# A delta-rule attention with a hard-swish MLP on one core: VectorE's order in the first five steps placed anew

## The chip, the core and the metric

The kernel runs on one core of a Trainium2 chip. The core has TensorE (PE; its weight loads are a row of their own, PEld), VectorE (DVE), ScalarE (ACT) and GpSimd (POOL), and DMA queues that here are issued from SyncE's queue (SP) and ScalarE's queue (ACTq). Each engine works its instructions off in the order of the program and waits for others by semaphores. The metric is the device time of one execution in microseconds (us).

## The reference

```python
def _attn_ref(q, k, v, beta):                 # B, H, S, D = 4, 8, 768, 48
    k_n = k / (np.linalg.norm(k, axis=-1, keepdims=True) + 1e-06)
    state = np.zeros((B, H, D, D))
    for t in range(S):
        y[:, :, t] = np.einsum('bhd,bhde->bhe', q[:, :, t], state)
        v_old = np.einsum('bhde,bhd->bhe', state, kt)
        state = state + bt * np.einsum('bhd,bhe->bhde', kt, vt - v_old)
    return y
def _moe_ref(x, w_in, w_out):                 # x is y as 3072 tokens x 384; d_ff = 2048
    h = x @ w_in
    g = h * np.clip(h + 3.0, 0.0, 6.0) / 6.0
    return g @ w_out
```

Inputs and output are 32-bit floats, but the two weight matrices arrive as 64-bit floats.

## The kernel before, in words

**Chunks.** The 768 steps of the recurrence are cut into 24 chunks t of 32 steps, and four chunks make a group g. A chunk holds 128 rows (4 batches x 32 steps) and all 8 heads. `norms(g, i0, n)` works out the inverse norms of n chunks: squares `sq` of k, a sum `ss` by VectorE, and 13 small VectorE operations (a seed, three Newton rounds, a reciprocal) up to `inv`. There is one buffer for `sq`, so a square waits for the sum of the one before. `prep(t)` has three stages: POOL makes `kb` (k times inv), the mask `mb` and `bkb`; PE transposes `kb` and then `qb` into PSUM (`pt`) and ACT copies each to `KQ`; PE makes the scores `sc` and VectorE multiplies them by `mb` to `LB`, which goes to `l_dram`. `inverse(g)` fetches the four chunks' triangles into `A`, inverts them in 30 steps on VectorE (a product `pr` and a subtraction into `A` in each), writes them to `x_dram` and fetches them back into the four `LB`. `chain(t)` is the serial part: `ks` and part of `py` from the state, `R` (VectorE), `pz`, `Z` (ACT), the rest of `py`, `y` (ACT), the update `su` with `state` (VectorE), and `yt`, which puts y transposed into `xT`.

**Weights.** w_in comes in 8 pieces of 256 columns, w_out in 8 pieces of 256 rows (0 to 7 and 8 to 15 below). A raw piece `d` is loaded by SP and made a 32-bit float by `convert` in five VectorE operations (`e`, `m`, `m`, `e`, and the last one into `w_in` or `w_out`) and one of ACT; each VectorE operation is a step that the program can place. Raw pieces and the k of a group share three buffers.

**MLP.** Two chunks make a block of 256 tokens. A unit of `up` is one of 16 column tiles: three products into `ph`, ACT's `t`, VectorE's `g`; one piece of w_in serves two units. A unit of `down` is two products into `po` by w_out. `ph`, `po`, `pt`, `pz` and `yt` share four PSUM buffers.

**Order.** Nothing reorders the work beyond the program's own order: under `manual_schedule` the loops at the end call the generators step by step (`take`, `drain`), and `need(n)` runs `convert` until n pieces are done. First come chunks 0 to 3 with `norms` of group 1 between them, then `inverse(0)` with the preparation of chunks 4 to 7 between its steps, then `chain(0)` and `chain(1)`. In the steps t = 2 and 3 each has 8 units of `up(0)`; in between lie `chain(t)` and `fill`, which is `norms(2)` and `inverse(1)`. From t = 4 on, `down` begins.

Of the kernel before, what the change touches and what calls it, by code (L numbers as in the profile page):

```python
# [17 lines left out]
def kernel(  # L18
# [28 lines left out]
    GS = 4  # L47
# [154 lines left out]
    def norms(g, i0, n):  # L202
# [3 lines left out]
        for i in range(n):  # L206
            sq = work.tile([P, H, D], FP32, name="sq", bufs=1)
            if g == 0:
                nc.scalar.activation(out=sq[:], in_=kf[:, i0 + i], func=ACTF.Square)
            else:  # L210
                nc.gpsimd.tensor_tensor(  # L211
                    out=sq[:], in0=kf[:, i0 + i], in1=kf[:, i0 + i], op=ALU.mult
                )
            nc.vector.tensor_reduce(out=ss[:, i, :], in_=sq[:], axis=AX.X, op=ALU.add)  # L214
            yield
# [277 lines left out]
    def mlp_units():  # L493


        u1 = up(1)
        yield from up(0)
        for f in range(0, NFC, WF):
            for c in range(CB):
                need(NWI + f // WF + 1)  # L500
                down(0, c, f, WF)
                yield
            for _ in range(WF):
                next(u1)
                yield
        for blk in range(1, N // CB):
            for c in range(CB):
                for f in range(0, NFC, 2):
                    down(blk, c, f, 2)
                    yield  # L510
            if blk + 1 < N // CB:
                yield from up(blk + 1)
# [27 lines left out]
    with tc.manual_schedule():  # L540
        with tc.tile_pool(name="early", bufs=3) as early:
# [5 lines left out]
            load_w(0, early)  # L547
# [7 lines left out]
            for t in range(1, GS):  # L555
# [3 lines left out]
                take(inv1, 3)  # L559
                take(first[t])  # L560
            drain(inv1)
            load_w(1, early)
            load_v(0)
            load_v(1)
            load_w(2, early)
            load_w(3)
            need(1)
            inv = inverse(0, nc.scalar)
            take(inv)
            for t in range(GS):  # L570
                take(prep_of(GS + t))
                take(inv, 4)
                take(prep_of(GS + t), 2)
                if t < 2:
                    take(prep_of(GS + t))
            load_w(4)
            take(inv, 4)
            take(conv)
            drain(inv)
            for t in range(2, GS):  # L580
                take(prep_of(GS + t))
            need(2)
# [6 lines left out]
            need(3)  # L589
# [3 lines left out]
        for t in range(CB, N):  # L593
# [29 lines left out]
            for u in range(NU):  # L623
# [4 lines left out]
                if early:  # L628
                    need(min(NWI, ((t - CB) * NU + u) // 4 + 1))
                else:  # L630
                    take(conv, 2)
                take(units)
                take(fill, 3 if early else 1 + (u % 2 == 0))
# [32 lines left out]
```

## Time and profile before

| what | value |
| --- | --- |
| median of 3 timed runs | 805.8 us (804.25 to 805.96) |
| the profiled execution's own time | 803.47 us |
| span of its trace | 801.8 us |
| PE busy in the span | 681.7 us (85%) |
| VectorE busy | 356.3 us (44%) |
| ScalarE busy, GpSimd busy | 181.9 us, 93.1 us |

The profiled execution took 1.67 us more than its trace spans, which is what lies around the first and the last instruction. PE is busy all the time from 245 us on; before that it has gaps.

### The profile page before, as it was taken

What the parts mean: (1) busy time and instruction counts of PE and PEld (TensorE: products, weight loads), DVE (VectorE), ACT (ScalarE), POOL (GpSimd) and SP (SyncE); (2) the same over time, 40 slices, a digit from 0 to 9 for tenths busy, and PEclk for the clock granted to TensorE, in tenths of its full rate; (3) what the DMA queues carried; (4) which work ended last, traced back from release to release, by engine and by line L of the source; (5) the groups of instructions that cost most, each with busy time, mean ns of one, the idle gap of its engine ahead of it and who ended that gap; (6) DMA issues with size and microseconds to landing.
All of it is one profiled execution on the core that took longest, in us unless ns stands there. A gap on an engine that the chain in (4) does not pass through costs nothing.

```text
span 801.8 us, 24917 instructions
## 1 busy us (share of the span) xinstructions
PE 681.7 (85%) x11208; PEld 502.7 (63%) x11208; DVE 356.3 (44%) x865; ACT 181.9 (23%) x357; POOL 93.1 (12%) x138
## 2 busy tenths in 40 slices
PE   0351483457879999999999999999999999999997
PEld 0341462335657687686786776876867768677684
DVE  3379547675862872136751248711366202112020
ACT  0221120122232032131131320322312203112120
POOL 2561012000300301004002012010000000000000
PEclk9996586578999999999999999999999999999999
DMA  6354651225742114250132330121201200000000
GB/s 120 72 121 103 146 109 32 74 72 125 211 80 46 39 23 83 42 110 8 30 69 40 62 71 12 47 46 38 52 12 48 38 14 19 8 17 1 20 1 20
DMA packets 140140, 45.77 MB, mean 57 GB/s; under 512 B 130273, under 2 KB 133345, under 8 KB 140033
## 3 DMA queue, kind: packets, MB, share of 16 engines
q1 hardware_dynamic: 127008, 41.18, 22.6%
q10 hardware_dynamic: 13024, 2.98, 1.8%
q8 instruction: 88, 1.44, 0.8%
q14 instruction: 20, 0.16, 0.1%
HBM read 33.13 MB, written 11.01 MB: 55 GB/s over the span
## 4 chain that ended last, share of the span: by engine, by line
PE 76%; DVE 13%; DMA 4%; SPq 2%; issue 2%; POOL 1%; ACT 1%; ACTq 0%; POOLq 0%; DVEq 0%
PE po L481 31%; PE ph L460 31%; DVE A L324 3%; DVE pr L320 3%; PE pz L372 2%; PE py L372 2%; PE su L429 2%; PE pt L275 2%; PE ks L362 2%; SPq L85 2%; PE sc L288 2%; PE py L362 1%; DMA qb<-in_q_dram 1%; DVE m L179 1%; DVE e L183 1%
## 5 line engine op out<-in xcount | busy, mean ns | idle before, releaser
L460 PE MATMUL ph<-xT,w_in 128*128 128x256 f32 x1152 | 278.8, 395 | 43.4 <-DVE w_in L188 36.9
L460 PEld LDWEIGHTS ph<-xT,w_in 128*128 128x128 f32 x1152 | 219.6, 196 | 78.2 <-DVE w_in L188 31.8
L481 PE MATMUL po<-w_out,g 128*128 128x384 f32 x768 | 265.1, 494 | 4.1 <-DVE w_out L188 4.1
L481 PEld LDWEIGHTS po<-w_out,g 128*128 128x128 f32 x768 | 141.5, 191 | 90.8 <-DVE w_out L188 4.6
L469 DVE SCALAR_TENSOR_TENSOR g<-t,ph 128x256 f32<-128x256 f32 x192 | 80.7, 420 | 207.9 <-ACT t L465 207.6
L465 ACT ACTIVATE t<-ph,half 128x256 f32<-128x256 f32 x192 | 91.2, 475 | 226.4 <-PE ph L460 212.7
L324 DVE TENSOR_TENSOR A<-A,pr 128x30 f32<-128x30 f32 (+9 forms) x180 | 67.9, 377 | 6.2
L320 DVE TENSOR_TENSOR pr<-A 128x30 f32<-128x30 f32 (+9 forms) x180 | 66.8, 371 | 5.9 <-DMA A<-l_dram 1.7
L437 DVE TENSOR_TENSOR state<-state,su 128x384 f32<-128x384 f32 x46 | 23.2, 547 | 73.3 <-PE su L429 73.3
L278 ACT ACTIVATE KQ<-pt 128x512 f32<-128x512 f32 x48 | 28.2, 597 | 87.4 <-PE pt L275 74.2
L253 POOL TENSOR_TENSOR kb<-kf,inv 128x384 f32<-128x384 f32 x24 | 20.3, 845 | 198.0 <-PE pt L275 157.0
L275 PE MATMUL pt<-ident,kb 128*128 128x128 f32 x96 | 18.0, 319 | 29.3 <-POOL kb L253 29.3
L260 POOL TENSOR_TENSOR mb<-beta_tok,mask 128x256 f32<-128x256 f32 x48 | 32.7, 701 | 75.4 <-DVE LB L294 75.4
L211 POOL TENSOR_TENSOR sq<-kf 128x384 f32<-128x384 f32 x20 | 17.0, 852 | 175.9 <-DMA kf<-in_k_dram 109.4
L487 ACT ACTIVATE o<-po 128x384 f32<-128x384 f32 x24 | 11.8, 492 | 111.5 <-PE po L481 111.5
L294 DVE TENSOR_TENSOR LB<-sc,mb 128x512 f32<-128x512 f32 x24 | 16.4, 685 | 46.3 <-PE sc L288 46.3
L275 PEld LDWEIGHTS pt<-ident,kb 128*128 128x128 f32 x96 | 13.5, 164 | 34.3 <-POOL kb L253 29.8
L288 PE MATMUL sc<-KQ 64*32 64x64 f32 x1536 | 22.8, 249 | 12.7 <-ACT KQ L278 12.6
L214 DVE TENSOR_REDUCE ss<-sq 128x8 f32<-128x384 f32 x24 | 13.3, 552 | 38.4 <-POOL sq L211 24.2
L388 DVE TENSOR_TENSOR R<-vf,ks 128x384 f32<-128x384 f32 x23 | 12.7, 551 | 37.1 <-PE ks L362 37.1
L288 PEld LDWEIGHTS sc<-KQ 64*32 64x32 f32 x1536 | 18.4, 117 | 16.6 <-ACT KQ L278 15.4
L372 PEld LDWEIGHTS py<-Z,LB 32*32 32x32 f32 x1536 | 19.5, 111 | 12.8 <-issue 11.2
(55 smaller groups left out, 401.5 us busy)
## 6 DMA issues: line engine op xcount, KB each, us to landing
d<-in_moe_w_in_dram SPq DMA_DIRECT2D x8, 768.0 KB, 4.9
d<-in_moe_w_out_dram SPq DMA_DIRECT2D x8, 768.0 KB, 5.2
kf<-in_k_dram SPq DMA_DIRECT2D x96, 48.0 KB, 2.3
vf<-in_v_dram SPq DMA_DIRECT2D x96, 48.0 KB, 2.2
out_dram<-o SPq DMA_DIRECT2D x96, 48.0 KB, 1.6
qb<-in_q_dram SPq DMA_DIRECT2D x80, 48.0 KB, 2.3
l_dram<-LB SPq DMA_DIRECT2D x20, 128.0 KB, 2.4
A<-l_dram SPq DMA_DIRECT2D x5, 512.0 KB, 3.8
```

Of the source, the lines that this page charges most:

```text
L260: nc.gpsimd.tensor_tensor(out=mb[:, e], in0=beta_tok[:, t, e:H:2].unsqueeze(2).unsqueeze(3).to_broadcast([P, NP, 2, C]), in1=mask2[:].unsq ...
L275: nc.tensor.transpose(pt[:, p, :], src[:, 2 * p : 2 * p + 2].rearrange("p e w -> p (e w)"), ident[:])
L278: nc.scalar.activation(out=KQ[:, :, j, :], in_=pt[:], func=ACTF.Copy)
L288: nc.tensor.matmul(scv[rows(b), e, p], lhsT=KQ[r, p, 0, rows(b)], rhs=KQ[r, p, :, rows(b)], start=True, stop=True,)
L320: nc.vector.tensor_tensor(out=pv, in0=A[:, j, j + 1 :].unsqueeze(1).to_broadcast([128, j, n]), in1=A[:, 0:j, j].unsqueeze(2).to_broadcast( ...
L324: nc.vector.tensor_tensor(out=A[:, 0:j, j + 1 :], in0=A[:, 0:j, j + 1 :], in1=pv, op=ALU.subtract)
L362: nc.tensor.matmul(ph[rows(b), e, D * p : D * p + D], lhsT=KQ[r, p, j, rows(b)], rhs=state[r, b, p, :], start=(p == 0), stop=True, skip_gr ...
L372: nc.tensor.matmul(place(h, b), lhsT=m(h)[rows(b)], rhs=z[rows(b), D * h : D * h + D], start=start, stop=True, skip_group_check=True, tile ...
L460: nc.tensor.matmul(ph[:], lhsT=w_in[:, s, f * 128 : (f + 1) * 128], rhs=xT[:, s, :], start=(s == 0), stop=(s == NKT - 1),)
L465: nc.scalar.activation(out=t1[:], in_=ph[:], func=ACTF.Relu, bias=half[:, 0:1], scale=1.0 / 6.0)
L469: nc.vector.scalar_tensor_tensor(out=g[:], in0=t1[:], scalar=1.0, in1=ph[:], op0=ALU.min, op1=ALU.mult)
L481: nc.tensor.matmul(po[:], lhsT=gs[blk, f][:, c * P : (c + 1) * P], rhs=w_out[:, f, :], start=(f == 0), stop=(f == NFC - 1),)
```

## The change

It touches five places. (1) The squares of group 0 no longer run on ACT: of each call of `norms(0, ...)` the first and third chunk go to VectorE, the second to POOL. (2) The raw pieces 0 to 2 are loaded right behind the k of groups 0 and 1. (3) In the first part, `norms(1)` stands as one block ahead of the scores of chunk 2, and three conversion steps stand between the scores of chunks 2 and 3; two pieces are converted before `inverse(0)` starts. (4) Of chunks 4 to 7, 4 is prepared before `inverse(0)`, 5 within it (its transposes before), and 6 and 7 behind it, with conversion steps between them. (5) In the MLP's first steps a piece is asked for one ahead of the units that use it (`+ 2` for `+ 1`), and in t = 2 and 3 three steps of `fill` stand ahead of each unit and no longer behind it.

```diff
@@ norms
-            if g == 0:
-                nc.scalar.activation(out=sq[:], in_=kf[:, i0 + i], func=ACTF.Square)
-            else:
-                nc.gpsimd.tensor_tensor(
-                    out=sq[:], in0=kf[:, i0 + i], in1=kf[:, i0 + i], op=ALU.mult
-                )
+            eng = nc.vector if g == 0 and i % 2 == 0 else nc.gpsimd
+            eng.tensor_tensor(
+                out=sq[:], in0=kf[:, i0 + i], in1=kf[:, i0 + i], op=ALU.mult
+            )
@@ mlp_units
-                need(NWI + f // WF + 1)
+                need(min(NW, NWI + f // WF + 2))
@@ the first part
-            load_w(0, early)
+            for i in range(3):
+                load_w(i, early)
...
                 take(first[t], 2)
-                take(inv1, 3)
+                if t == 2:
+                    drain(inv1)
+                if t == 3:
+                    take(conv, 3)
                 take(first[t])
-            drain(inv1)
-            load_w(1, early)
             load_v(0)
             load_v(1)
-            load_w(2, early)
             load_w(3)
-            need(1)
             inv = inverse(0, nc.scalar)
             take(inv)
-            for t in range(GS):
-                take(prep_of(GS + t))
-                take(inv, 4)
-                take(prep_of(GS + t), 2)
-                if t < 2:
-                    take(prep_of(GS + t))
+            need(2)
+            for t in range(2):
+                take(prep_of(GS + t), 3)
+            take(prep_of(GS))
+            take(inv, 10)
+            take(prep_of(GS + 1))
             load_w(4)
-            take(inv, 4)
+            take(inv, 12)
             take(conv)
             drain(inv)
+            take(prep_of(GS + 2), 2)
+            take(conv)
+            take(prep_of(GS + 3), 2)
+            take(conv)
             for t in range(2, GS):
-                take(prep_of(GS + t))
-            need(2)
+                take(prep_of(GS + t), 2)
+                take(conv)
...
-            need(3)
+            need(4)
@@ the loop over t
                 if early:
-                    need(min(NWI, ((t - CB) * NU + u) // 4 + 1))
+                    need(min(NWI, ((t - CB) * NU + u) // 4 + 2))
                 else:
                     take(conv, 2)
+                if early:
+                    take(fill, 3)
                 take(units)
-                take(fill, 3 if early else 1 + (u % 2 == 0))
+                if not early:
+                    take(fill, 1 + (u % 2 == 0))
```

Line numbers behind line 213 are two lower in the changed kernel. VectorE's first instructions, up to the first inverse norm, stood so before (`sq` comes from ACT here):

```order
L135 MEMSET rebias 128x1
L122 STREAM_TRANSPOSE beta_tok<-beta_hm 128x768
L214 TENSOR_REDUCE ss<-sq 128x8
L217 TENSOR_SCALAR seed<-ss 128x8
L224 SCALAR_TENSOR_TENSOR nt<-ss,seed 128x8
```

With the change the square is VectorE's own, and the transpose of beta stands behind the seed instead of ahead of the sum:

```order
L135 MEMSET rebias 128x1
L209 TENSOR_TENSOR sq<-kf 128x384
L212 TENSOR_REDUCE ss<-sq 128x8
L215 TENSOR_SCALAR seed<-ss 128x8
L122 STREAM_TRANSPOSE beta_tok<-beta_hm 128x768
L222 SCALAR_TENSOR_TENSOR nt<-ss,seed 128x8
```

ScalarE's queue around `inverse(0)`, from the load of `A` to the first `Z` of `chain(0)`, was before (each `KQ` is a copy of transposed k or q, two a chunk):

```order
L311 DMA A<-l_dram_321 128x1024
L278 ACTIVATE KQ<-pt 128x4x128 x8
L169 ACTIVATE e<-e,rebias 128x768
L329 DMA x_dram_322<-A 128x1024
L335 DMA LB<-x_dram_322 128x8x32 x4
L400 ACTIVATE Z<-pz 128x384
```

With the change four of these copies, those of chunks 6 and 7, stand behind the five DMA issues:

```order
L309 DMA A<-l_dram_325 128x1024
L169 ACTIVATE e<-e,rebias 128x768
L276 ACTIVATE KQ<-pt 128x4x128 x4
L169 ACTIVATE e<-e,rebias 128x768
L327 DMA x_dram_326<-A 128x1024
L333 DMA LB<-x_dram_326 128x8x32 x4
L276 ACTIVATE KQ<-pt 128x4x128 x4
L398 ACTIVATE Z<-pz 128x384
```

VectorE at the start of t = 3, from the chain's `R` on, was before (the five operations are those of piece 4, which the unit of this `g` uses):

```order
L388 TENSOR_TENSOR R<-vf,ks 128x2x4x48
L168 TENSOR_SCALAR e<-d 128x768
L173 TENSOR_SCALAR m<-d 128x768
L179 SCALAR_TENSOR_TENSOR m<-d,m 128x768
L183 SCALAR_TENSOR_TENSOR e<-d,e 128x768
L188 SCALAR_TENSOR_TENSOR w_in<-m,e 128x3x256
L469 SCALAR_TENSOR_TENSOR g<-t_1650,ph 128x256
L320 TENSOR_TENSOR pr<-A 128x240
```

With the change the five are those of piece 5, the next one's, and three steps of the inverse stand between them and the `g`:

```order
L386 TENSOR_TENSOR R<-vf,ks 128x2x4x48
L168 TENSOR_SCALAR e<-d 128x768
L173 TENSOR_SCALAR m<-d 128x768
L179 SCALAR_TENSOR_TENSOR m<-d,m 128x768
L183 SCALAR_TENSOR_TENSOR e<-d,e 128x768
L188 SCALAR_TENSOR_TENSOR w_in<-m,e 128x3x256
L318 TENSOR_TENSOR pr<-A 128x240
L322 TENSOR_TENSOR A<-A,pr 128x16x15
L318 TENSOR_TENSOR pr<-A 128x238
L322 TENSOR_TENSOR A<-A,pr 128x17x14
L318 TENSOR_TENSOR pr<-A 128x234
L322 TENSOR_TENSOR A<-A,pr 128x18x13
```

PE's order is the same but for chunks 5 to 7: the scores of 4 follow the transposes of 5, and the scores of 6 and 7 with the transpose of q of 7 are the last things ahead of `chain(0)`'s `pz`.

## Rows read from the trace of the kernel before

**Rows 1.** Busy us (instructions) of each engine by stretch; PEclk is the granted clock.
```profile
106.40:187.40 81.00, 43.46 (x720) 33.74 (x717) 51.76 (x122) 15.29 (x28) 9.65 (x13) 0.73 0.29 81
245.00:801.80 556.80, 552.45 (x8385) 403.56 (x8383) 202.89 (x526) 130.04 (x268) 42.60 (x59) 1.00 0.17 36
```
**Rows 2.** Waits of DVE, 106.4 to 187.5 us: total, times, longest.
```profile
DVE g L469 <- ACT t L465: 21.5, 8, 3.7
DVE ss L214 <- POOL sq L211: 5.2, 4, 2.5
```
**Rows 3.** Waits of PE, 106.4 to 191.9 us.
```profile
PE ph L460 <- DVE w_in L188: 36.9, 5, 12.9
```
**Rows 4.** Timeline of the start: start, length, engine, line, operation, [idle before <-releaser].
```profile
1.74 1.56 SPq L85 DMA_DIRECT2D kf<-in_k_dram  x3
...
3.87 9.59 ACTq L90 DMA_DIRECT2D qb<-in_q_dram  x15
...
5.57 0.98 DVE L122 STREAM_TRANSPOSE beta_tok<-beta_hm 128x768 f32<-128x768 f32 x1 [1.04 <-DMA qb<-in_q_dram]
...
13.62 1.28 ACT L209 ACT_TABLE_LOAD   x1 [13.62 <-DMA kf<-in_k_dram]
...
15.47 0.55 DVE L214 TENSOR_REDUCE ss<-sq 128x8 f32<-128x384 f32 x1 [8.92 <-ACT sq L209]
...
18.47 0.20 DVE L240 RECIPROCAL inv<-nt 128x8 f32<-128x8 f32 x1
```
**Rows 5.** Issues to landing, the page's part 6 (KB each, median us).
```profile
d<-in_moe_w_in_dram SPq DMA_DIRECT2D x8, 768.0 KB, 4.9
...
kf<-in_k_dram SPq DMA_DIRECT2D x96, 48.0 KB, 2.3
```
**Rows 6.** Timeline, 28 to 56 us.
```profile
29.39 1.19 POOL L260 TENSOR_TENSOR mb<-beta_tok,mask 128x256 f32<-128x256 f32 x2
...
34.05 0.83 POOL L211 TENSOR_TENSOR sq<-kf 128x384 f32<-128x384 f32 x1
...
39.51 1.09 ACT L278 ACTIVATE KQ<-pt 128x512 f32<-128x512 f32 x2 [7.42 <-DVE LB L294]
...
46.26 1.18 PE L288 MATMUL sc<-KQ 64*32 64x64 f32 x64 [2.53 <-ACT KQ L278]
...
47.37 1.11 PE L275 MATMUL pt<-ident,kb 128*128 128x128 f32 x4
47.48 0.69 DVE L294 TENSOR_TENSOR LB<-sc,mb 128x512 f32<-128x512 f32 x1 [1.45 <-PE sc L288]
...
52.56 1.26 DVE L188 SCALAR_TENSOR_TENSOR w_in<-m,e 128x768 f32<-128x768 f32 x1
...
55.53 0.19 DVE L320 TENSOR_TENSOR pr<-A 128x30 f32<-128x30 f32 x1 [1.72 <-DMA A<-l_dram]
```
**Rows 7.** Timeline, 81 to 88 us.
```profile
81.57 0.34 ACTq L329 DMA_DIRECT2D x_dram<-A  x1
...
84.23 3.08 ACTq L335 DMA_DIRECT2D LB<-x_dram  x4
...
87.08 1.50 PE L372 MATMUL pz<-vf,LB 32*32 32x48 f32 x64 [22.18 <-DMA LB<-x_dram]
```
**Rows 8.** Timeline, 101 to 188 us.
```profile
101.75 11.47 SPq L85 DMA_DIRECT2D kf<-in_k_dram  x16
...
106.47 0.55 DVE L388 TENSOR_TENSOR R<-vf,ks 128x384 f32<-128x384 f32 x1
...
140.96 0.55 DVE L168 TENSOR_SCALAR e<-d 128x768 uint32<-128x768 uint32 x1
...
144.89 5.49 PE L460 MATMUL ph<-xT,w_in 128*128 128x256 f32 x12 [6.66 <-DVE w_in L188]
...
180.24 0.96 DVE L188 SCALAR_TENSOR_TENSOR w_in<-m,e 128x768 f32<-128x768 f32 x1
...
187.41 0.55 DVE L388 TENSOR_TENSOR R<-vf,ks 128x384 f32<-128x384 f32 x1 [0.18 <-PE ks L362]
```

## The prediction

> **What bounds the kernel now.** I read the stretches first. From 245 us to the end PE is busy 552 of 557 us at the full granted clock [rows 1]. The change touches nothing there, and its products and their order stay. So the end moves by as much as the time at which PE gets to its steady work, and the place to look is what precedes it. In the steps t = 2 and 3 (106 to 187 us) PE is busy 43 of 81 us and the mean granted clock is 0.73, between the 0.5 of 1.2 GHz and the 1 of 2.4 GHz. PE's waits there are nearly one kind: 36.9 us for the last conversion operation of a w_in piece [rows 3]. The reader may then take VectorE for the limit, but its own waits say otherwise: it stood 21.5 us for ACT's `t`, eight times, and 5.2 us for POOL's squares [rows 2]. The two wait for each other in turn. VectorE converts piece n, PE starts on it, VectorE's next instruction in the queue is the `g` of that very product and stands until it comes; then it does three steps of the inverse and only then the next piece, while PE stands. The start of a product after such a pause is slow as well: 5.49 us for two units [rows 8].
>
> The stage before that, up to 106 us, is a serial chain: norms, scores, the inverse on VectorE, a round trip through DRAM, `chain(0)`, `chain(1)`. There I read the timeline for what each link waits for.
>
> **Part 1, up to `chain(0)`: 8 us won, 5.3 lost again.** The first sum waited 8.92 us for ACT's square, and ACT began only at 13.62, right behind its own 15 loads of q, which end at 3.87 + 9.59 = 13.46 [rows 4]. The row names a load of k as what ACT waited for, but SP issued the third, fourth and fifth of its loads of k from 1.74 to 3.30, a chunk has four, and one lands in 2.3 [rows 4, 5], so I take 5 us. VectorE can then square at 5.0. Square 0.55 (an equal-sized VectorE operation, `R` [rows 8]), the transpose of beta, which now stands in this path, 1.0, the sum and 13 small operations as before 18.67 - 15.47 = 3.2: `inv` at 9.75, where it was 18.67. The table load stays hidden behind ACT's issues (to 14.9). POOL's `kb`, masks and `bkb` (0.83 + 1.19 + 0.83, the first and last sized as its square [rows 6]) put its square at 12.6; 0.83, sum 0.6, VectorE's square and sum 1.2, and 13 operations, 2.6 above and a little longer for three chunks, 2.9: their norms are there at about 18.2.
>
> Then two things give part of it back. POOL's squares of group 1 now come as four in a row behind `bkb` of chunk 3: each with its sum takes 1.5 us, and the block of 13 operations 3. POOL has three chunks of 2.85 to do from 18.2 on, of which the mask of the third waits for `LB` of chunk 1: squares from 26.6 to 32.5, the last `inv` of group 1 at 35.5. `LB` of chunk 2 is placed behind it (36.2), ACT's `KQ` of chunk 3 stands behind that `LB`'s DMA issue as it did before (7.42 us [rows 6]), its two copies end at 37.9, and the scores give `LB` of chunk 3 at 39.5 to 40 instead of 47.48: **-8.0**. The conversion steps that now lie around it run beside POOL's `kb`, and beside POOL the last operation of piece 0 took 1.26 us, against 0.96 alone for piece 7 [rows 6, 8]; I allow 0.5 for it. `A` follows 8.05 us behind the `LB` (55.53 - 47.48). In that gap VectorE ends piece 0 (2 us), does piece 1 (3.9 alone) and `LB` of chunk 4 (0.7): 6.6, or 7.5 beside POOL. It fits.
>
> The inverse took 26.0 us with two `LB` in it; now there is one, -0.7. So `x_dram` goes at 72.9 instead of 81.57. Here the change costs something. ACT issues the four loads of `LB` until 84.23 + 3.08 = 87.31, 5.74 us behind `x_dram` [rows 7], and the copies of chunks 6 and 7 now stand behind them in its queue: free at 78.6. Three copies 1.7 us, then scores of 6 (1.1), transpose of q of 7 (1.15), its copy (0.65), scores of 7 (1.1), all from the starts in [rows 6], bring `pz` of `chain(0)` to 84.4. Without this queue it would be 78.3, when the loads have landed. Against 87.08: **-2.7**. The two chains are as long as before, 106.47 - 87.08 = 19.4; the conversion steps in them have VectorE's idle time as cover. `R` of t = 2 is at 103.8.
>
> **Part 2, from `R` of t = 2 to `R` of t = 4: 25.2 us.** Before, 187.41 - 106.47 = 80.9, of which VectorE waited 26.9 [rows 2] (with 0.2 for `ks`). That leaves 54.0 of work with its gaps. With the change one of four pieces lies ahead of this stretch (-3.9 us, 144.89 - 140.96 for piece 4). What still waits:
> - The squares. The loads of k of group 2 took 11.47 us from 101.75. They stand on SP behind `LB` of chunk 7 (85.2), 8 loads of v and that of piece 5: at 0.72 a load (11.47 / 16) from 92.4 to 103.9. The first sum finds its square ready, the other three are paced by POOL, 1.5 us for 0.55 of work: about 3.2 us of wait.
> - The `g`s. Each has now a piece and three fill steps ahead of it, six us or more after its product became possible; a unit begun slowly takes 5.49 / 2 = 2.75 and 0.5 for `t`. All covered but the last: behind piece 7 no further w_in piece is asked for, and PE does two units, two transposes and `ks` in 187.41 - 181.2 = 6.2 us, beside which VectorE has 3.9 of work. Wait 2.3.
> Sum 54.0 - 3.9 + 3.2 + 2.3 = 55.6. `R` of t = 4 comes at 159.4 instead of 187.41.
>
> If PE ran all 16 units and both chains at 1.2 GHz, that would be 44 us and about 15: 59, or 3.5 more than VectorE's sum. That is the upper bound of this term; I take 0, since most gaps get shorter.
>
> **Part 3, behind it: 0.5 us lost.** Two pieces of w_out are converted ahead of the next `g`, and piece 10, the third, is now asked for before it has landed: its load stands on SP behind `x_dram` (155.1, two us behind piece 7), the loads of `LB` (5.74) and 8 of q and v (5.8), goes at about 166.7 and takes 4.9 [rows 5]. VectorE reaches it at 159.9 + 7.8 = 167.7 and waits 3.9. PE has its first `down` products and two units of `up` as cover for most of this. Both ends: 0, and the whole of piece and wait, 7.8. I take 0.5: by the lengths before, PE is at the third unit, which needs that `g`'s buffer, at about the time of the `g`.
>
> **Sum.** -2.7 - 25.2 + 0.5 = -27.4. On the profiled execution's 803.47 us that is 776.1. The median of the runs is 805.8, 2.3 above it; I set 778.
>
> **A rule that speaks against it.** Beside POOL the operation of piece 0 took a third longer (1.26 against 0.96 [rows 6, 8]); it slowed and went on. The Trainium skill (SBUF — State Buffer, SBUF: two separate sides) says that the port pair that VectorE and GpSimd share is an exclusive lock, which a VectorE operation with two SBUF inputs holds against a GpSimd operation that reads SBUF, "the other fully blocks". By this rule of the Trainium skill each POOL operation beside a conversion could cost VectorE its full length, and the sum would be 4.3 us higher, as the first rival works out; the row agrees that the two hinder each other, not that one waits out the other.
>
> **The rivals.**
> - *VectorE and POOL take turns to the full length.* The POOL operations of chunks 4 and 5 beside pieces 0 and 1 (2 x 2.85) cost 5.7 instead of the 1.4 allowed above: +4.3, **782**. For it: the slow operation of piece 0. Against: it was slowed by 0.3 and not by the 0.83 of a POOL operation. The lock of the Trainium skill (SBUF — State Buffer, SBUF: two separate sides) would give this rival.
> - *k lands late.* If the row of 13.62 is right that ACT waited for k, the start wins 0.1 and not 9: +8.9, **787**. For it: the releaser in the row. Against: SP's fifth load of k waits for the first and was out by 3.5 us.
> - *ACT's queue holds nothing.* If the copies of 6 and 7 get through ahead of the loads' wait, `pz` is at 78.3: -6, **772**. For it: the transposes are there 20 us earlier. Against: the 7.42 us of [rows 6], a copy behind a DMA issue.
> - *PE's slow starts keep the turns.* If at three of four pieces VectorE still stands 3.6 us for `g`, +10.8: **789**. For it: the 5.49 us; against: six us of work are put ahead of each `g`.
> - *Slower: a piece asked for one ahead stands a whole load.* The raw piece n+2 can only be loaded when n has left its buffer, and VectorE's queue stands at the first operation, with `g`, `state` and `LB` behind it. If each of the eight w_out pieces costs 4.9 us [rows 5]: +39, **817**. It turns slower than before from 28 / 8 = 3.5 us a piece on. For it: piece 10 in my own count; against: VectorE waits for no raw piece before [rows 2], and in the w_out stage PE has some 7 us of products a piece.
> - *It doesn't do what it says*: the requests ahead are already met by the conversion steps taken elsewhere, and the wait moves to `down`: **806**.
>
> **How the numbers follow.** Chances: forecast 0.52, take turns 0.07, k late 0.10, ACT's queue free 0.10, slow starts 0.13, a load each 0.05, no effect 0.03. The forecast's own range is 773 to 784: down by half of the queue's 6 and by small terms, up by 3.5 for PE's clock and some of the 7.3 left of part 3. The range 769 to 791 takes in all but the last two cases and the edges of k late and slow starts. A difference under 0.2% (1.6 us) is about what a measurement of this kernel can't tell from none: faster 0.92, same 0.03, slower 0.05.
>
> **What would show it.** Right: the first `sq` on VectorE at about 5 us and `inv` before 11; `x_dram` at about 73; `pz` waits for the scores of chunk 7 and not for the loads of `LB`, with the copies of 6 and 7 at 78 to 83; between `R` of t = 2 and of t = 4 less than 8 us of VectorE's waits for `t`, and PE's 36.9 for w_in under 15; the first `po` at about 164. Wrong: a wait of `e` or `m` for `d` at more than one piece, `pz` at 87 or later, or VectorE's waits for `t` still over 15 us. The prediction falls too if PE has new gaps behind 245 us.

## The result, and the profile after it

The changed kernel takes 778.6 us (median of 4 runs, 777.8 to 779.7) against 805.0 us of the kernel before (4 runs, 803.9 to 806.0): ratio 0.9673, 95% interval 0.9653 to 0.9694. The forecast was 778.0, range 769 to 791.

The profiled execution took 779.7 us, the longest of the four, with a span of 778.0; the one of before, 803.5, lies below all four of its runs. So the traces differ by 23.8 us of span, the medians by 26.4.

The page of the kernel after: two engines of its first part and three rows of the slices.

```profile
PE 681.3 (88%) x11208; PEld 501.7 (64%) x11208; DVE 359.1 (46%) x868; ACT 178.0 (23%) x353; POOL 94.8 (12%) x139
...
PE   1440686668799999999999999999999999999997
...
DVE  6498459968527831247711367511464213021020
...
PEclk9755577789999999999999999999999999999999
```

PE's work is what it was (681 us); the steady part has moved to the left. Its busy time by stretch, cut at `R` of t = 2 (104.9), of t = 4 (159.4) and of t = 5 (205.4); PEclk is the granted clock:

```profile
0.00:104.90 104.90, 38.84 (x1222) 31.18 (x1222) 68.59 (x167) 17.36 (x28) 34.80 (x60) 0.65 0.58 125
104.90:159.40 54.50, 41.05 (x723) 32.20 (x714) 47.25 (x117) 13.39 (x27) 8.83 (x12) 0.79 0.29 87
159.40:205.40 46.00, 33.15 (x570) 22.80 (x561) 37.21 (x53) 13.71 (x23) 7.78 (x7) 0.93 0.56 144
205.40:778.00 572.60, 568.28 (x8750) 415.49 (x8736) 206.10 (x533) 133.56 (x275) 43.44 (x60) 1.00 0.18 37
```

The second row answers to [rows 1]: 54.5 us where it was 81, and VectorE busy 47 of them. Two of VectorE's waits in this stretch and then the largest of PE's (total, times, longest):

```profile
DVE ss L212 <- POOL sq L209: 2.5, 3, 0.9
DVE g L467 <- ACT t L463: 2.2, 1, 2.2
```

```profile
PE ph L458 <- DVE w_in L188: 9.0, 3, 3.0
```

VectorE's 21.5 us for `t` [rows 2] are 2.2, PE's 36.9 for w_in [rows 3] are 9.0. VectorE now works through; it is the limit there.

The start, from the timeline (start, length, engine, line, operation, [idle before <-releaser]); it answers to [rows 4, 6, 7, 8]:

```profile
5.13 0.56 DVE L209 TENSOR_TENSOR sq<-kf 128x384 f32<-128x384 f32 x1 [0.59 <-DMA kf<-in_k_dram]
...
9.55 0.20 DVE L238 RECIPROCAL inv<-nt 128x8 f32<-128x8 f32 x1
...
39.10 0.68 DVE L292 TENSOR_TENSOR LB<-sc,mb 128x512 f32<-128x512 f32 x1
...
76.88 2.41 ACTq L333 DMA_DIRECT2D LB<-x_dram  x4
79.33 1.57 ACT L276 ACTIVATE KQ<-pt 128x512 f32<-128x512 f32 x3 [9.13 <-DMA LB<-x_dram]
83.23 0.60 ACT L276 ACTIVATE KQ<-pt 128x512 f32<-128x512 f32 x1 [2.32 <-PE pt L273]
...
84.99 1.50 PE L370 MATMUL pz<-vf,LB 32*32 32x48 f32 x64
```

The first `inv` is 9 us earlier, `LB` of chunk 3 8.4 us, `x_dram` goes at 74.23 instead of 81.57, and `pz` of `chain(0)` starts only 2.1 us earlier: ACT's copies of chunks 6 and 7 stand between, behind the four loads of `LB`.

**Where the 23.8 us come from.** The table gives the start of `R` in each step, from the timelines of VectorE, for all kernels of this study. (`y_norms_early` comes last among the experiments.)

| kernel | R t=2 | R t=3 | R t=4 | R t=5 | span | span less R t=5 | ratio of the runs to before, 95% |
|---|---|---|---|---|---|---|---|
| before | 106.47 | 140.49 | 187.41 | 229.45 | 801.8 | 572.4 | |
| after | 104.93 | 131.00 | 159.43 | 205.42 | 778.0 | 572.6 | 0.9673 (0.9653 to 0.9694) |
| a_ahead_only | 104.84 | 140.11 | 168.46 | 214.28 | 786.6 | 572.3 | 0.9817 (0.9786 to 0.9848) |
| b_start_only | 104.42 | 132.24 | 177.09 | 219.28 | 791.6 | 572.3 | 0.9851 (0.9822 to 0.9879) |
| c_fill_behind | 103.48 | 131.13 | 159.56 | 206.27 | 778.7 | 572.4 | 0.9706 (0.9674 to 0.9739) |
| f_not_ahead | 104.05 | 129.23 | 168.22 | 210.45 | 782.8 | 572.4 | 0.9784 (0.9749 to 0.9819) |
| d_wout_late | 104.66 | 130.70 | 157.48 | 202.28 | 774.8 | 572.5 | 0.9638 (0.9593 to 0.9682) |
| e_copies_first | 97.62 | 127.34 | 157.02 | 200.88 | 773.2 | 572.3 | 0.9630 (0.9588 to 0.9673) |
| g_act_squares | 115.46 | 141.50 | 168.29 | 214.39 | 786.7 | 572.3 | 0.9809 (0.9757 to 0.9861) |
| h_inverse_early | 97.74 | 130.68 | 157.47 | 206.19 | 778.7 | 572.5 | 0.9691 (0.9649 to 0.9734) |
| x1_four_buffers | 98.55 | 126.93 | 155.34 | 201.52 | 775.0 | 573.5 | 0.9648 (0.9625 to 0.9671) |
| x2_load_earlier | 96.83 | 126.58 | 155.00 | 198.69 | 771.9 | 573.2 | 0.9597 (0.9572 to 0.9623) |
| x3_late_too | 97.67 | 124.32 | 153.87 | 197.51 | 769.9 | 572.4 | 0.9572 (0.9547 to 0.9596) |
| y_norms_early | 101.16 | 126.34 | 147.42 | 189.35 | 761.7 | 572.4 | 0.9489 (0.9451 to 0.9526) |

From `R` of t = 5 on every kernel takes 572.3 to 573.5 us. So the reading that PE's steady work is only moved holds, and each microsecond can be placed: -1.5 up to `R` of t = 2, -26.4 from there to `R` of t = 4 (80.94 to 54.50), **+4.0** from there to `R` of t = 5 (42.04 to 45.99), +0.2 behind. Sum -23.8.

### The profile page after: what moved, and what is told of

The parts are those of the page before. It is cut to its first block, busy times and chain, and to the rows that moved or that the text cites. A ratio compares the mean times of both kernels' runs of the same rounds, so it can differ in the third digit from the quotient of the medians.

```text
span 778.0 us, 24919 instructions
## 1 busy us (share of the span) xinstructions
PE 681.3 (88%) x11208; PEld 501.7 (64%) x11208; DVE 359.1 (46%) x868; ACT 178.0 (23%) x353; POOL 94.8 (12%) x139
## 4 chain that ended last, share of the span: by engine, by line
PE 74%; DVE 14%; DMA 4%; issue 3%; SPq 2%; POOL 2%; ACT 1%; ACTq 0%; POOLq 0%; DVEq 0%
PE po L479 31%; PE ph L458 29%; DVE A L322 3%; DVE pr L318 3%; PE pz L370 2%; PE py L370 2%; PE su L427 2%; PE sc L286 2%; PE ks L360 2%; PE pt L273 2%; DMA kf<-in_k_dram 2%; PE py L360 2%; DVE m L179 1%; DVE e L183 1%; DVE e L168 1%
## 5 line engine op out<-in xcount | busy, mean ns | idle before, releaser
L276 ACT ACTIVATE KQ<-pt 128x512 f32<-128x512 f32 x48 | 27.8, 596 | 84.5 <-PE pt L273 64.4
L292 DVE TENSOR_TENSOR LB<-sc,mb 128x512 f32<-128x512 f32 x24 | 16.4, 685 | 57.3 <-PE sc L286 57.3
L169 ACT ACTIVATE e<-e,rebias 128x768 uint32<-128x768 uint32 x16 | 15.0, 935 | 80.9 <-DVE e L168 80.9
```

The lines of the kernel that those rows point to most:

```text
L276: nc.scalar.activation(out=KQ[:, :, j, :], in_=pt[:], func=ACTF.Copy)
```

## The experiments

Times are the medians of each kernel's runs; the kernel before is run beside each group (803.6 us for the first four, 804.1 for the next four, 804.3 and 804.5 for the last ones).

**The change taken apart: start, requests ahead, fill steps.** My theory was that of the prediction; the rival came from the trace of after, where PE stood 3 us at each piece of t = 3 until the piece converted *ahead* was done. It could be that a product waits for the newest piece, whichever it reads; then the order of the fill steps, and not the request ahead, would be what helps.

`a_ahead_only` is the kernel before with these lines of the change; `b_start_only` is the kernel after without them. `c_fill_behind` takes only the last hunk out of the kernel after, `f_not_ahead` only the first.

```diff
-                    need(min(NWI, ((t - CB) * NU + u) // 4 + 1))
+                    need(min(NWI, ((t - CB) * NU + u) // 4 + 2))
...
-                need(NWI + f // WF + 1)
+                need(min(NW, NWI + f // WF + 2))
...
+                if early:
+                    take(fill, 3)
                 take(units)
-                take(fill, 3 if early else 1 + (u % 2 == 0))
+                if not early:
+                    take(fill, 1 + (u % 2 == 0))
```

> The kernel before with only the requests one piece ahead and the fill steps ahead of the units; the start stays as it was. By the prediction's sum (parts add up, part 2 and 3 alone are -25.2 + 0.5): 805 - 25 = 780. By cycles (each piece that is still converted in t = 2 and 3 costs what it adds to VectorE's queue, and four instead of three lie there, 3.9 us more than in the kernel after): R of t = 4 at 106.5 + 54.5 + 3.9 = 164.9, five and a half behind the kernel after, 784. If the early start is needed for it (loads of k or of the raw pieces late): 790 or more.

> The kernel after with the early start only: requests not ahead, fill steps behind the units. By the prediction's sum (part 1 is -2.7, one piece less in t = 2 and 3 is -3.9): 805 - 6.6 = 798. By cycles (a piece that leaves t = 2 and 3 takes its whole turn with it, 13.1 us from piece to piece before, of which 6.2 is fill work that stays; t = 2 then holds no turn at all, t = 3 has three and the last operation of a fourth): about 8 to 12 less than before for the stretch and 1.5 for the start, 792 to 795; then the parts don't add up.

> The kernel after with the fill steps behind the units again; the requests stay one ahead. If the request ahead makes a product possible before the next conversion, as the prediction says, each g has a whole conversion (3.9 us) as cover and little is lost: 778.6 to 780, VectorE's waits for t in t = 3 under 4 us. The trace of the kernel after speaks against it: PE stood 2.91, 3.05 and 3.02 us in t = 3 until the last operation of the piece that was converted ahead, which its product does not read. If a product waits for the newest piece, g stands first behind it again as before, three times 3.0 to 3.6 us: 787 to 790, with three waits for t of some 3.6 us.

> The kernel after with the w_in pieces converted just before their product again; the fill steps stay ahead of the units. If the request ahead is what gives the gain, this loses most of it: each turn waits again, 785 to 790. If a product waits for the newest piece in any case, the order of VectorE's queue is the same but for one piece's place, and the time is that of the kernel after within 3 us, 777 to 782, with a longer wait behind the last piece.

Measured: 789.5, 792.9, 780.5 and 787.3 us. `a_ahead_only` misses both sums (780 and 784) and comes out next to the third case, that the early start is needed (790 or more): its way from `R` of t = 2 to `R` of t = 4 is 63.6 us where 58.4 was expected, and the 5.2 us between are VectorE's sums, which wait 7.7 us for POOL's squares instead of the 2.5 of after. `b_start_only` comes out as the count by cycles has it: the prediction books the piece that leaves t = 2 at 3.9 us, the stretch wins 8.3. So the prediction's terms hold for the whole change and not for its halves.

VectorE's waits for `t` from 103 to 178 us, in the kernels with the early start: neither half, requests ahead alone, fill steps ahead alone.

```profile
DVE g L467 <- ACT t L463: 19.9, 7, 3.7
```

```profile
DVE g L467 <- ACT t L463: 3.7, 2, 2.2
```

```profile
DVE g L467 <- ACT t L463: 11.4, 6, 3.6
```

The rival falls. `c_fill_behind` has the fill steps behind the units, and no `g` of t = 3 waits except the last; its `R` of t = 4 is at 159.56, that of after at 159.43. Its timeline at piece 5 shows why PE stands all the same:

```profile
126.45 4.72 PE L458 MATMUL ph<-xT,w_in 128*128 128x256 f32 x12
...
131.73 0.88 PE L370 MATMUL pz<-R,LB 32*32 32x48 f32 x64 [0.56 <-DVE R L386]
...
134.51 0.96 DVE L188 SCALAR_TENSOR_TENSOR w_in<-m,e 128x768 f32<-128x768 f32 x1
135.38 0.41 DVE L467 SCALAR_TENSOR_TENSOR g<-t,ph 128x256 f32<-128x256 f32 x1
135.52 2.86 PE L458 MATMUL ph<-xT,w_in 128*128 128x256 f32 x12 [2.91 <-DVE w_in L188]
```

PE had done both units of piece 4 by `R` (131.13); what it waits for at 135.5 is piece 5, and that is the piece its next product reads. The `g` behind the conversion, at 135.38, belongs to a unit of 126 to 131 and finds its `t` ready. PE is ahead of VectorE's queue and starves for conversions: with the request ahead it waits for VectorE, and VectorE no longer waits for PE.

The four kernels also show which part of the change acts where. Step t = 3 takes 46.9 us before, 44.9 with the start alone, 28.4 with the requests alone, 28.4 with both. Step t = 2 takes 34.0 before, 27.8 with the start alone (no conversion and no turn lies in it any more, and the sums wait 2.5 us for squares instead of 5.2), 35.3 with the requests alone (a whole piece lies in it, and the sums wait 7.7 us), 26.1 with both. So the gains sit in different steps, and they add up: ratios of 0.9851 and 0.9817 multiply to 0.967, the ratio of after is 0.9673. Within part 2 they do not: of t = 3, with the early start, the fill steps alone win 5.9 us (38.99), the request alone 16.4, both no more.

**The tail: the request ahead for w_out.** `d_wout_late` asks for the w_out pieces one at a time.

```diff
-                need(min(NW, NWI + f // WF + 2))
+                need(NWI + f // WF + 1)
```

> The kernel after with the w_out pieces (8 to 15) requested one at a time again, w_in still one ahead. In the kernel after the stretch from R of t = 4 to the end took 618.6 us, before 614.4: piece 10 was asked for 3.0 us before its load had landed, VectorE's g and ACT's copies stood behind it, PE lost 2.6 us at pz and ran at a lower clock after the next gap. If that is the cause, R of t = 4 stays at 159.4, the wait of e for d goes, and the time is 774.4. If the longer tail has another cause, it stays at 778.6. If w_out needs the piece ahead, PE's waits of po for w_out grow past the 4.0 and it is slower than 779.

Measured: 776.1 us, between the two cases (774.4 and 778.6). First the longest waits of the kernel after between `R` of t = 4 and t = 5, of PE and of VectorE:

```profile
PE ph L458 <- ACT KQ L276: 4.1, 2, 3.1
PE po L479 <- DVE w_out L188: 4.0, 1, 4.0
...
PE pz L370 <- ACT KQ L276: 2.6, 1, 2.6
...
PE ph L458 <- ACT xT L417: 1.0, 1, 1.0
...
PE sc L286 <- issue: 0.7, 1, 0.7
```

```profile
DVE e L168 <- DMA d<-in_moe_w_out_dram: 3.0, 1, 3.0
```

The first two and that for `xT` stand in the kernel before as well (4.1, 4.1 and 1.0). In `d_wout_late` `e` waits for no load and `pz` not at all; between the two `R` it takes 44.8 us instead of 46.0, not the 42.0 of before. The rest lies in the clock; its stretches (columns as above):

```profile
157.50:172.50 15.00, 11.02 (x209) 7.30 (x194) 8.95 (x13) 3.43 (x5) 0.64 (x1) 0.77 0.56 116
172.50:202.30 29.80, 23.65 (x361) 16.56 (x364) 24.54 (x37) 9.65 (x17) 7.13 (x7) 0.94 0.63 168
```

PE was busy 34.7 us for what took 32.0 in the same stretch of before (187.4 to 229.5, where the clock was 0.89 and then 1.00). PE stood idle 12.85 us of this stretch in after, 10.13 in `d_wout_late` and 10.06 before. So the waits are shown as the request's, 2.7 us of PE's time; the other part comes from the granted clock, which was lower in these traces for reasons that the rows don't give. In the medians the kernel is 2.5 us faster than after, with intervals that overlap.

**The start.** `g_act_squares` puts the squares of group 0 back on ACT. `e_copies_first` takes the transposes and copies of chunks 6 and 7 ahead of the end of the inverse. `h_inverse_early` also moves the norms of group 1 behind `LB` of chunk 3, and pieces 0 and 1 behind `x_dram`.

The edit of `g_act_squares`:

```diff
-            eng = nc.vector if g == 0 and i % 2 == 0 else nc.gpsimd
-            eng.tensor_tensor(
-                out=sq[:], in0=kf[:, i0 + i], in1=kf[:, i0 + i], op=ALU.mult
-            )
+            if g == 0:
+                nc.scalar.activation(out=sq[:], in_=kf[:, i0 + i], func=ACTF.Square)
+            else:
+                nc.gpsimd.tensor_tensor(
+                    out=sq[:], in0=kf[:, i0 + i], in1=kf[:, i0 + i], op=ALU.mult
+                )
```

That of `e_copies_first`:

```diff
             take(conv)
+            for t in range(2, GS):
+                take(prep_of(GS + t), 3)
             drain(inv)
-            take(prep_of(GS + 2), 2)
-            take(conv)
-            take(prep_of(GS + 3), 2)
-            take(conv)
+            take(conv, 2)
             for t in range(2, GS):
-                take(prep_of(GS + t), 2)
+                take(prep_of(GS + t))
                 take(conv)
```

And the core of `h_inverse_early`, which also takes two conversion steps instead of one at each step of the two chains:

```diff
-                if t == 2:
-                    drain(inv1)
-                if t == 3:
-                    take(conv, 3)
...
             take(inv)
-            need(2)
+            drain(inv1)
```

> The kernel after with the squares of group 0 on ACT as before, behind its 15 loads of q. If the 8.9 us by which the first inv came earlier carry through the whole start, the first inv is back at about 18.5, LB of chunk 3 at about 48, x_dram at about 82.5, and the time is 786.5 to 787.5. If POOL's squares of group 1 or the loads set the start anyway, x_dram moves by less than 3 us and the time stays under 782.

> The kernel after with the transposes and copies of chunks 6 and 7 placed ahead of the last steps of the inverse, so that ACT has them done before it stands for x_dram. If ACT's queue is what puts pz of chain(0) at 84.99 (copies at 79.33 and 83.23 behind the four loads of LB that end at 79.29), pz comes at about 79.5 when LB has landed, everything behind it 5.5 us earlier, 773. If the loads of LB themselves, or k of group 2 behind them, set the time, pz or the first sum of group 2 waits for a DMA and less than 2 us is won.

> The kernel after with the norms of group 1 behind LB of chunks 2 and 3 instead of ahead of them, in the gap in which A makes its way through DRAM, the pieces 0 and 1 moved from that gap to VectorE's idle time behind x_dram and in chain(0) and chain(1) (17 us idle in the kernel after), and the copies of chunks 6 and 7 early as well. If LB of chunk 3 waits for nothing but the norms placed ahead of it: LB of chunk 3 at about 30.5 instead of 39.1, the first step of the inverse at about 39.5 instead of 48.5, x_dram at about 66, pz at 71, R of t = 2 at 91: 765. If the two pieces don't fit into the idle time, their 7.8 us come back: 772. If loads (raw pieces, k of group 2) come too late for it, VectorE's e or ss waits for a DMA and less than 5 us is won.

Measured: 788.9, 774.9 and 780.0 us. `g_act_squares`: the first `inv` at 18.59, `x_dram` at 84.85, `R` of t = 2 at 115.46. What the squares win at 10 us, 9.0 there, arrives at the end: 8.7 us in the traces, 10.3 by the medians, more than the 786.5 to 787.5 us expected.

`e_copies_first`: `pz` waits for `LB` alone, 5.5 us earlier than in after, as its theory says. The second and third row show where that stops: k of group 2 is loaded when it was loaded before, and the sums wait for it.

```profile
79.54 1.50 PE L370 MATMUL pz<-vf,LB 32*32 32x48 f32 x64 [6.10 <-DMA LB<-x_dram]
...
92.60 10.94 SPq L85 DMA_DIRECT2D kf<-in_k_dram  x16
...
104.34 0.55 DVE L212 TENSOR_REDUCE ss<-sq 128x8 f32<-128x384 f32 x1 [2.40 <-POOL sq L209]
```

`R` of t = 2 is 7.3 us earlier, of t = 3 3.7, and 3.7 is what the medians show, with intervals that overlap.

`h_inverse_early`: `LB` of chunk 3 at 29.83 and the first step of the inverse at 40.16, within a microsecond of what was expected, `x_dram` at 68.94. Then the two pieces stand in the way of the chains (`R` at 97.74 instead of 91), k of group 2 comes at 96.86, after 5.7 us of waiting for VectorE's last read of piece 3, whose buffer it takes, and VectorE's sums wait 10.2 us. At `R` of t = 3 nothing is left of a start that was 9 us ahead; piece 10 is even later (`e` waits 4.5 us), and the time is that of after, not the 765 expected. The theory of the link was right, the gain went into the next one.

**What holds k of group 2.** In after its first load went (93.20) as soon as VectorE had read piece 3 (93.17), whose buffer it takes. In `e_copies_first` that read ended at 87.80, and the load went at 92.60 all the same. `x1_four_buffers` gives the tag a fourth buffer, on top of `e_copies_first`. `x2_load_earlier` also loads the raw pieces from the seventh on one piece sooner, and `x3_late_too` takes the request ahead for w_out out again (as in `d_wout_late`).

```diff
-                kfs[g] = stage.tile([P, GS, H, D], FP32, name="kf", tag="d", bufs=3)
+                kfs[g] = stage.tile([P, GS, H, D], FP32, name="kf", tag="d", bufs=4)
...
-        raws[i] = pool.tile([128, dst.shape[1], dst.shape[2], 2], U32, name="d", tag="d", bufs=3)
+        raws[i] = pool.tile([128, dst.shape[1], dst.shape[2], 2], U32, name="d", tag="d", bufs=4)
```

The second edit, in `convert`:

```diff
-            if i + 2 not in raws and i + 2 > 4:
-                load_w(i + 2)
+            for n in (i + 2, i + 3):
+                if n > 4 and n not in asked and (n == i + 2 or i > 3):
+                    asked.add(n)
+                    load_w(n)
```

> The kernel with the copies of chunks 6 and 7 early (e_copies_first) and four buffers instead of three under the tag d, which the groups of k and the raw pieces share. With three, k of group 2 took the buffer of piece 3: its loads went at 92.6 to 103.5 in both kernels, as soon as piece 3 had been read, while R of t = 2 had moved from 104.9 to 97.6, and VectorE's sums of group 2 waited 6.1 us instead of 2.5. If that buffer is what held the rest of the gain back, the loads of k go from about 86 to 96, the sums wait 2.5 to 3.5 us, R of t = 3 is at about 123.7 and R of t = 4 at 150.5 to 152, and the time is 768.5 to 772. If the DMA queues themselves are what is late (k, v and the raw piece together), k still lands after 103 and it stays at 774 to 775.

> The kernel before this one (x1_four_buffers) with each raw piece from the seventh on loaded three pieces ahead instead of two, so that the load of piece 10 stands on SP ahead of x_dram and the loads of LB, q and v. If the wait for piece 10 causes the longer tail, e waits for no load, pz of t = 4 doesn't wait, and from R of t = 4 to the end it is 614 to 616 us: 2 to 3 us less than x1_four_buffers, 766 to 769. If the tail is the granted clock's alone, the same as x1_four_buffers.

> x2_load_earlier with the w_out pieces requested one at a time again. If the request ahead for w_out is worth nothing once it waits for no load, the same time within 1 us. If it is worth something, PE's waits of po for w_out exceed 4.2 us and it is slower by more than 1 us; if it only keeps VectorE's g back, faster by 1 to 2.

Measured: 776.4, 772.7 and 770.9 us. The buffer was not it: with four, the loads of k start at 91.40 instead of 92.60, and the time is that of `e_copies_first`. For the longer tail the loads of piece 10 were the cause: in `x2_load_earlier` `e` waits for no load, `pz` of t = 4 not for ACT, and `R` of t = 4 to t = 5 takes 43.7 us instead of 46.2; the time is 3.7 us less than that of `x1_four_buffers`, though not the 766 to 769 expected. `x3_late_too` is 1.8 us below it, with overlapping intervals; its t = 2 was shorter as well (26.7 against 29.8), so what the request ahead for w_out is worth by then stays open.

SP's own waits, 50 to 106 us, in the kernel after, name what k stands behind:

```profile
SPq L90 <- DMA LB<-x_dram: 17.9, 1, 17.9
```

One load of q, for chunk 10, stood from 61 to 79.4 us until ACT's loads of `LB` had landed; behind it in SP's queue are `LB` of chunks 6 and 7, v, piece 5 and k. `y_norms_early` asks for k ahead of that load, for q of chunks 10 and 11 after the chains, lets SP issue `x_dram` and its loads, and takes the norms of group 2 in `chain(0)` and `chain(1)`, where VectorE was idle. It stands on `x3_late_too`; the lines that move q and `x_dram` are not shown.

```diff
-                take(prep_of(GS + t), 3)
+                take(prep_of(GS + t))
+            for n in range(GS):
+                load_k(2 * GS + n)
+            for t in range(2, GS):
+                take(prep_of(GS + t), 2)
             drain(inv)
+            fill = chained(norms(2, 0, GS), inverse(1, nc.sync))
...
             for t in range(CB):
                 load_v(t + 2)
-                for _ in chain(t):
+                for i, _ in enumerate(chain(t)):
                     take(conv)
+                    take(fill, 1 if t * 4 + i < 9 else 0)
```

> x3_late_too with SP's queue cleared of what held k of group 2: in all kernels so far SP stood 17.8 to 18.8 us at a load of q for chunk 10 until ACT's loads of LB had landed (79.4), and LB of chunks 6 and 7, v, the raw piece and k of group 2 stood behind it. Here k of group 2 is asked for ahead of that, the loads of q for chunks 10 and 11 come after it, SP issues x_dram and the loads of LB itself, and the norms of group 2 and the load of A of the second inverse are taken in chain(0) and chain(1), where VectorE stood 10 us. If SP's queue was the cause, k goes from about 60 to 72, no sum of group 2 waits at t = 2, and the 5.3 us of norms and 3 us of waits leave t = 2 and 3: R of t = 2 at about 97.5, R of t = 4 at 146 to 148, 762 to 765. If PE at its lower clock sets t = 2 and 3 by now, R of t = 4 comes at 150 to 153 and the time is 767 to 770. If x_dram behind the loads of k is late, R of t = 2 comes after 100 and nothing is won: 770 to 774.

Measured: **765.2 us** (6 runs, 761.4 to 766.2), ratio 0.9489 (0.9451 to 0.9526) to before: below both kernels and all others here. The trace:

```profile
61.04 9.60 SPq L85 DMA_DIRECT2D kf<-in_k_dram  x16
...
79.77 1.50 PE L374 MATMUL pz<-vf,LB 32*32 32x48 f32 x64 [6.03 <-issue]
...
90.47 1.50 PE L374 MATMUL pz<-R,LB 32*32 32x48 f32 x64 [1.13 <-DVE R L390]
...
94.78 1.19 PE L374 MATMUL py<-Z,LB 32*32 32x48 f32 x49 [1.60 <-issue]
...
101.16 0.54 DVE L390 TENSOR_TENSOR R<-vf,ks 128x384 f32<-128x384 f32 x1
...
147.42 0.55 DVE L390 TENSOR_TENSOR R<-vf,ks 128x384 f32<-128x384 f32 x1 [0.25 <-PE ks L364]
```

k is there 30 us sooner, no sum waits in t = 2, and t = 2 with t = 3 takes 46.3 us where `x3_late_too` took 56.2 and after 54.5. `R` of t = 2 came at 101.2 and not at 97.5. The largest differences to `x3_late_too` (97.67): `pz` of `chain(0)` starts 0.8 us later (78.93 there), PE makes a longer pause by 1.3 (0.33 there; see the last section), and `pz` of `chain(1)` waits 1.1 for an `R` that stood behind the norms. From `R` of t = 4 to t = 5 it takes 41.9, as before. The run moves the loads of k and the norms together, so what either is worth alone stays open.

## Why the prediction was right, step by step

- **PE's steady work only moves.** Shown by the 572.3 to 573.5 us behind `R` of t = 5 in all fourteen traces.
- **k is there at 5 us.** `sq` started at 5.13 (forecast 5.0) and `inv` was there at 9.75, as forecast. The rival that k lands late falls, and `g_act_squares` shows the price of this step, 10.3 us by the medians and 8.7 in the traces, where the rival said 8.9.
- **The chain to `x_dram`.** Last `inv` of group 1 forecast at 35.5, ended at 35.6; `LB` of chunk 3 at 39.5 to 40, started at 39.1; `x_dram` at 72.9, went at 74.2. The difference is VectorE beside POOL: I allowed 1.4 us for pieces 0 and 1, they took 11.4 us instead of 7.9, so the inverse began at 48.5 and not at 47.6, and it took 25.8 us instead of 25.3. The rival of turns to the full length has the mechanism right, as shown below, and its size too high, 5.7 where 3.5 were lost.
- **ACT's queue.** `pz` forecast at 84.4, came at 84.99, right behind the scores of chunk 7; `e_copies_first` shows that the queue is the cause. What it would bring at the end was mis-sized in the rival: 6 us, and 3.7 arrived, since k of group 2 ends the wait next.
- **`chain(0)` and `chain(1)`, 19.4 us.** They took 19.9, with a pause of PE of 2.8 us in them that was 1.4 before (see the last section). Part 1 is -1.5 in this trace and -1.5 to -3.0 in five traces with the same start (`R` of t = 2 at 103.5 to 104.9), against -2.7.
- **Part 2, -25.2** (the sum of 55.6 against 80.9 gives -25.3). Measured -26.4: the sum of VectorE's work and what still waits, 55.6 forecast, 54.5 found. The terms hold one by one: 2.2 for the last `g` (2.3 forecast), 2.5 for the squares (3.2), no other `g` waits. One reason given was too generous: "a piece and three fill steps ahead of it"; the piece alone is enough (`c_fill_behind`), the three fill steps alone are not (`f_not_ahead`). The rival of PE's slow starts falls.
- **Part 3 is the term that was mis-sized.** Forecast +0.5, measured +4.0 between `R` of t = 4 and t = 5. The wait itself was there as worked out: VectorE reached piece 10 at 167.7, as forecast, and stood 3.0 us (3.9 forecast). The step that failed is the cover: "PE has its first `down` products and two units of `up` as cover". ACT's `e` of piece 10 stood ahead of the copy of a transpose, and `pz` waited for that copy, 2.6 us. Of the 4.0, PE's idle time makes up 2.8 and a lower clock 1.2 (PE busy 33.1 us instead of 32.0). It is also the slower rival's mechanism at one piece of eight, not a loss that turns the sign.
- **The total.** Parts 1, 2 and 3 came out at -1.5, -26.4 and +4.0 where -2.7, -25.2 and +0.5 stood: errors of +1.2, -1.2 and +3.5, in the traces -23.8 instead of -27.4. In the medians it is -26.4, since the profiled run of after was its slowest and that of before faster than its other runs; and 778 was set 1.9 above the sum. So the median meets the forecast closer than the terms do.

**The rule that spoke against it.** The prediction read its row of before as both engines slowing down and going on. The ends of the operations show that they take turns. VectorE's operations of piece 1 and POOL's beside them in after:

```profile
42.99 0.97 DVE L173 TENSOR_SCALAR m<-d 128x768 uint32<-128x768 uint32 x1
43.51 1.14 POOL L264 TENSOR_TENSOR bkb<-kb,beta_tok 128x384 f32<-128x384 f32 x1
43.99 1.47 DVE L179 SCALAR_TENSOR_TENSOR m<-d,m 128x768 f32<-128x768 uint32 x1
44.61 1.54 POOL L251 TENSOR_TENSOR kb<-kf,inv 128x384 f32<-128x384 f32 x1
45.39 1.58 DVE L183 SCALAR_TENSOR_TENSOR e<-d,e 128x768 uint32<-128x768 uint32 x1
47.00 0.96 DVE L188 SCALAR_TENSOR_TENSOR w_in<-m,e 128x768 f32<-128x768 f32 x1
```

The length of a row holds its wait. Alone the three of VectorE that have another beside them take 0.55, 0.96 and 0.95 us, those of POOL 0.83. The first `m` ends at 43.96, `bkb` 0.69 later, the next `m` 0.81 behind `bkb`, `kb` 0.69 behind that, `e` 0.82 behind `kb`: each ends somewhat less than its own length after the other engine's, and the last, with nothing beside it, takes its 0.96. In the fourteen traces all 91 of the conversions' SCALAR_TENSOR_TENSOR operations that began while one of POOL ran end 0.81 to 0.82 us after it. `LB`, one of whose inputs is the scores in PSUM, takes 0.68 beside POOL's `bkb` (39.10 above) as it does alone. The row that the prediction read was such a turn too. POOL's masks beside it, in before:

```profile
50.39 2.61 POOL L260 TENSOR_TENSOR mb<-beta_tok,mask 128x256 f32<-128x256 f32 x2
```

They end at 53.00, and the operation of 52.56 [rows 6] ends 0.82 later: its extra 0.3 us were the rest of a mask.

The Trainium skill (SBUF — State Buffer, SBUF: two separate sides) says of the port pair that the two share that "the other fully blocks". The trace agrees, with the ends 0.69 and 0.81 us apart. VectorE's ten conversion operations lost 3.5 us, between the 1.4 that I allowed and the 5.7 of the rival, because each of them stood only for what was left of one POOL operation, 0.03 to 0.63 us.

## What to carry to other kernels

When two engines wait for each other in turn, putting one more unit of independent work ahead of the instruction that closes the turn breaks it, and one such cover is enough: a second on top brought nothing. A start that gets shorter hands its gain to the next link, so ask what that link's loads stand behind in their queue; here both further changes to the start stopped at loads of k that were issued hardly earlier (92.60) or later (96.86) than in after (93.20), and moving these loads, together with the norms that use them, won more than the links themselves (6 us against 4 and none). Cover has to be followed through every queue that a late instruction blocks: the wait for one raw piece cost most not on VectorE but through ACT's queue, on PE. And where two engines hinder each other, compare the ends of their operations and not only the lengths: constant distances between the ends tell that one waits for the other.

## What I had not expected of the hardware

- **A queue that waits for another engine's transfers.** SP stood 17.9 us at a load of q until ACT's loads of `LB` had landed (18.8 in `e_copies_first`, 17.8 in `x3_late_too`; in `h_inverse_early` 17.1 until `x_dram` had), though that load uses neither their data nor their buffer. In the program's list of waits that load of q and the first of the loads of `LB` wait on the same one of eight semaphores, which would explain it; the semaphore was not tried by itself, only that k gets through when it stands ahead.
- **The same products at either clock.** The two units behind piece 5 start after the same 2.9 us of wait in after and in `c_fill_behind`; the twelve products took 5.49 us there and 2.86 here, at 1.2 and at 2.4 GHz. The mean granted clock over the last 30 us before `R` of t = 4 was 0.75 in one and 0.82 in the other. What PE did before was alike (twelve products of 4.99 and 4.72 us, `pz` of 0.88), so the rows don't tell which level comes.
- **PE's pauses end when a block of instructions has landed.** In the middle of `py` of `chain(1)`, among 64 equal products, PE stood 2.79 us in after, 1.43 before, 2.19 in `d_wout_late`, 1.05 in `e_copies_first`, put down to "issue". The trace also has the DMA packets of a queue that the page calls `q8 instruction`, 16 KB each. In after one of them ran from 96.63 to 97.78 us, and PE went on at 99.20. The row of the pause, and that of the queue in part 3 of the page of after (packets, MB, share):

```profile
99.20 1.19 PE L370 MATMUL py<-Z,LB 32*32 32x48 f32 x49 [2.79 <-issue]
```

```profile
q8 instruction: 88, 1.44, 0.8%
```

Of PE's 32 pauses of 0.5 us or more that are put down to "issue" in the fourteen traces, 30 end 1.3 to 1.7 us behind the end of such a packet; the other two are `pz` of `chain(0)`, which waits for `LB`. So the rows say that PE stood for its next instructions; no run moved these packets. The pauses shift `R` of t = 2 by a microsecond or two between kernels with the same start.
